# One of two raw quads through an accumulating DMA, with pairwise minima in SBUF, in an attention and gated FFN kernel on one Trainium2 core

## The chip, the cores and the metric

The kernel runs on one core of one Trainium2 chip. The metric is the device time of one execution in microseconds (us). The core's engines are named as in the profile: PE is TensorE (PEld its weight loads), DVE is VectorE, ACT is ScalarE, POOL is GpSimd, and SP issues most DMAs.

## What is computed

`x` has 2048 rows of 448 columns. Two blocks read the same `x` and are mixed by a gate of one number per row (float32 throughout):

```python
g = sigmoid((x * gate_w).sum(-1, keepdims=True))
q, k, v = split(x @ wqkv)              # 16 heads of 28
p = softmax(q @ k.T * 28 ** -0.5)      # per head, 2048 x 2048
a = (p @ v) @ wo
gate, up = x @ W_gate, x @ W_up        # 448 -> 1792
b = (relu(gate) * up) @ W_down
out = g * a + (1 - g) * b
```

## The kernel before

**Precision.** A float32 operand of the projections is split into a high part (a copy rounded to the fast matmul type, `act_high`, L102) and a low part (the rest, a subtraction: `low` on VectorE, L108, or `pool_low` on GpSimd, L111). Eleven matmuls per projection tile multiply the parts. Q and K are kept as high and low rows of one 128-row tile, together with two rows that carry a subtracted maximum.

**Stages.** A prologue computes Q, K and V (Q and K go through DRAM, `qk_d`). Then come 32 *visits* v, two per head h = v // 2, each for half of the 16 key chunks of 128 and all four query blocks of 512. Beside the attention of a visit runs a part of the FFN's gate and up projections. After the visits the rest of the FFN, the output projection and the down projection follow.

**Two ways of taking the softmax maximum.** Scores are computed transposed, keys on the partitions. For query blocks 0 to 2 the row maximum of the scores is found beforehand: `smax` (L161) computes a score tile with queries on the partitions into a PSUM pair of 128x1024 (L169), and VectorE reduces it (L171). `smax_end` (L178) transposes a head's maxima and writes them into two rows of its Q tile, so that later scores come out of TensorE with the maximum already subtracted; ScalarE evicts them by an exponential (L260). Heads are 1.5 ahead: the first m of an odd visit 2h+1 is the first that reads Q and K of head h+2. Query block 3 has no maximum beforehand. Its scores are *raw*: in each visit the first four score pairs (two *quads* of 128x2048 in SBUF) are copied raw by ScalarE (L262). `block_max` (L211) takes their elementwise maximum on VectorE, reading the PSUM pair itself, in 512-column operations (L228) into a tile `RM`. `all_max` (L232) reduces `RM` over the partitions on GpSimd (L234), `take_max` (L237) subtracts it from one quad on VectorE (L239), and `take_exp` (L242) takes the quad's exponential on ScalarE (L246). For an odd visit `RM` starts from the even visit's, and `rescale` (L574) corrects the head's even half.

**The order within a visit** is written out by hand as a string, one letter a step, and every engine executes its instructions in this order:

- s: one score pair, two matmuls (L256) and its eviction; m: one `smax` step, two matmuls and a reduction; x: one gate or up matmul (L547), 11 of them to a unit, with `relu` (L557), the product (L560) and a spill at a unit's end, and `load_f` (L536) for split weights after every second unit
- A: `all_max`; d: `take_max`; e: `take_exp`; c, f: the two parts of `rescale`; n: `smax_end` in odd visits
- w: the split of raw FFN weights that the next visits need (`split_f`, L519; 14 blocks in two parts each, so only in the early visits), with the low parts on GpSimd; u, l: special steps of the first visit
- P, Q: the two halves of the product with V (`pv`, L593), 32 matmuls each (L601), called the po block here

FIRST is the string of visit 0 (2 units), LONG of most (3 units, 33 x), WIDE has 4 units (44 x), LATE is that of the last three visits, with 4 units and no m. The scores run three pairs ahead of the visit (AHEAD), so the fourth raw pair of a visit is scored behind the po block of the visit before. Eight early scores lie in the prologue; their maxima are taken in one loop after it (L660). PSUM has three pairs for s and m together, and two single banks.

**Other queues.** `small_things` (L638) is called at a visit's start and at its eighth s. At the start of even visits it loads K and Q of head h+2 (`load_k` L146, `load_q` L151, four DMAs of 224 KB each, over SP); at the eighth s of even visits it inverts the row sums of the head before (`row_sums` L613, through `l_d` in DRAM) and spreads them back over partitions (`spread` L619, `rb`); at the start of odd visits it normalises (`normalise` L625). SP's queue is in program order: a DMA that waits holds back those behind it.

Of the kernel before, what the change touches and what calls it, by code (L numbers as in the profile page):

```python
# [37 lines left out]

EARLY = (5, 4, 4, 3, 2, 2, 1, 1)

AHEAD = 3

NP = 10

FIRST = "AmxmxsmxmxxlxsxumsmmmxxxsxdxxxsxssmxxmxsmmxdexxsxsewsPQ"

LONG = "ssmnAxxxxsmxsxmxsmxxxmsmxxxsmxxmxsdxsxxxsxsmxxxsmxxmexxsmxxdxxcsxsefwsPQ"

WIDE = "smnmxxxxxxxsxxmxxxxmsxmxxsmxxsAmxsxmxxsxsmxdxsxxsssxxxmxxxcsxmsxxdxxmxxxxexsxewsPfQ"

LATE = "snwsxxAxdxxxsxxsxxxsxxdsxxxxcsxxsxxxsxxxsxxxxsxsxxxxsxxxxxexxxsxxessPfQ"
# [15 lines left out]
def gated_mix_kernel(ctx, tc, x, wq, wo, wgu, wd, out):  # L67
# [8 lines left out]
    def f32(ap):  # L76
        return ap.bitcast(F32)
# [21 lines left out]
    def ps_x(name):  # L99
        return psum.tile([P, TB], F32, tag="x", bufs=2, name=name)  # L100
# [105 lines left out]

    stream = [p for v in range(2 * H) for p in visit(v)]
    todo_max, todo_sub, todo_exp, todo_all = [], [], [], []
    RM = {}

    def block_max(v, j, k, p, q):  # L211

        n = TQ[v // 2]
        b = j - NB + n
        if (v, b) not in RM:
            if b == 0:
                rm = att.tile([P, max(TQ), TB], F32, name=f"rm_{v}", tag=f"rm{v % 2}", bufs=1)
                for c in range(n):
                    RM[v, c] = rm[:, c]
        r = RM[v, b]  # L220
        if k % (NK // 2):
            parts = [(p[:, c], r) for c in range(2)]
        elif v % 2:
            parts = [(p[:, 0], RM[v - 1, b]), (p[:, 1], r)]
        else:
            parts = [(p[:, 0], q[:, 1])]
        for x, y in parts:
            nc.vector.tensor_tensor(r, x, y, op=OP.max)  # L228
        if k % (NK // 2) == NK // 2 - 2:
            todo_all.append((v, b, [(v, j, i) for i in (k // 4 - 1, k // 4)]))  # L230

    def all_max():  # L232
        v, b, quads = todo_all.pop(0)
        nc.gpsimd.partition_all_reduce(RM[v, b], RM[v, b], P, bass_isa.ReduceOp.max)  # L234
        todo_sub.extend((v, b, q) for q in quads)

    def take_max():  # L237
        v, b, q = todo_sub.pop(0)
        nc.vector.tensor_tensor(QUAD[q], QUAD[q], RM[v, b].unsqueeze(1).to_broadcast([P, 4, TB]), op=OP.subtract)  # L239
# [8 lines left out]
    def score(late=True):  # L248

        v, done, q, half, chunks = stream.pop(0)  # L250
        h = v // 2
        if q not in QUAD:
            QUAD[q] = p_slot(next(slots) % NP, f"P_{v}_{q[1]}_{q[2]}")
        ps = ps_w(f"s_{v}_{chunks[0][0]}_{chunks[0][1]}")
        for c, (k, j) in enumerate(chunks):
            nc.tensor.matmul(ps[:, c], K[h % 3][:, k * P:(k + 1) * P], Q[h][:, j * TB:(j + 1) * TB], start=True, stop=True)  # L256
            AT[v, k, j] = QUAD[q][:, 2 * half + c]
        dst = QUAD[q][:, 2 * half:2 * half + 2]
        if done:
            nc.scalar.activation(dst, ps, AF.Exp, scale=SCALE)  # L260
        else:
            nc.scalar.activation(dst, ps, AF.Copy)  # L262
# [25 lines left out]
    with tc.tile_pool(name="qkv", bufs=1) as pa:  # L288
# [132 lines left out]

        warm = pa.tile([P, TB], BF16, name="warm")
        nc.vector.memset(warm, 0.0)
        ps = ps_x("warm_ps")
# [51 lines left out]
        for n, (f, *a) in enumerate(mixed):  # L476
            if n == 0:
                split_w(*w5)
            if n == 6:
                load_k(1)  # L480
                load_q(1)
            if n == 8:
                split_w(*w3)
            if n == 13:

                nc.gpsimd.memset(f32(K[2])[96:128], -1.0)
            if n == len(mixed) - 6:
# [8 lines left out]
            news = [(score, False) for back in EARLY if back == len(mixed) - n]  # L496
# [161 lines left out]
    split_f(0, act_high, pool_low, (0,))  # L658
    fetch_f(1)
    while todo_max:  # L660
        block_max(*todo_max.pop(0))
    for v, (order, nu) in enumerate(ROUNDS):
        todo = list(range(nxt, nxt + nu))
        nxt += nu
        small_things(2 * v)
        passes = [(*divmod(k, 2), n) for k in todo for n in range(NT)]
        units = []
        ns = 0
        for o in order:
            if o == "x" and not passes:  # L670
                continue
            if o == "s":
                ns += 1
                if ns == 8:
                    small_things(2 * v + 1)
                if stream:
                    score()
            elif o == "m":
                if m < len(maxima):
                    smax(m)  # L680
                    m += 1
            elif o == "x":
                i, half, n = passes.pop(0)
                if n == 0:
                    units.append((i, half, ps_x(f"gu_{i}_{half}")))
                gu_mm(units[-1][2], i, half, n)
                if n == NT - 1:
                    i, half, ps = units.pop()
                    spill_h(i, ps) if half else relu(i, ps)
                    if half:  # L690
                        load_f(i + 2)
            elif o == "n":
                if v % 2 and v < 2 * H - 1:
                    smax_end(v // 2 + 1)
            elif o == "w":
                ready = nxt + (ROUNDS[v + 1][1] if v + 1 < len(ROUNDS) else 2)
                ready = min(ready + ready % 2, 2 * NF)
                while parts < ready:
                    split_f(parts // 2, act_high, pool_low, (parts % 2,))
                    parts += 1  # L700
                    if parts % 2 == 0:
                        fetch_f(parts // 2 + 1)
            elif o == "A":
                all_max()
            elif o == "d":
                take_max()
            elif o == "e":
                take_exp()
            elif o in "cf":
                rescale(v, "cf".index(o))  # L710
            elif o == "l":
                sends.pop()()
            elif o == "u":
                split_f(0, act_high, pool_low, (1,))
# [8 lines left out]
        left = [k for k in todo_exp + todo_sub + todo_all if k[0] == v]  # L723
        assert not passes and not left and v not in PO or len(stream) == max(0, 16 * (2 * H - 1 - v) - AHEAD), (v, passes, left, len(stream) + 16 * (v + 1))
    assert not stream and m == len(maxima), (len(stream), m)
    stk.close()

# [181 lines left out]
```

## Time and profile before

| | us |
|---|---|
| median of 3 runs | 1289.12 (1284.76 to 1290.27) |
| the profiled execution | 1281.88 |
| its span, first to last instruction | 1280.1 |
| prologue, up to the first steps of FIRST | 0 to about 120 |
| end of the prologue, FIRST up to its po block | 120 to 170 |
| from the first po block to the last | 170.3 to 1065.8 |
| rest of the FFN, output and down projection | from 1074 |

Durations below come from the profiled execution. A row of the grouped view reads: line, engine, operation, output<-input, shape, xcount | busy us, mean ns of one | idle time of the engine before them and what ended it. The chain is the work that ended last, followed back from the end: a start, a length and an instruction in each row. A row of the stretch view reads: stretch, length, busy us of PE, PEld, DVE, ACT, POOL with instruction counts, granted TensorE clock, DMA share, GB/s. "issue" is time in which an engine waited for nothing that the profile shows.

### The profile page before, as it was taken

To read this page: it belongs to the slowest core of one execution; us is meant where nothing else is said; L and a number is where in the kernel's file an instruction comes from. 1 tells how busy PE (TensorE), PEld (TensorE's weight loads), DVE (VectorE), ACT (ScalarE), POOL (GpSimd) and SP (SyncE) were. 2 spreads that over 40 slices of the span, in tenths; PEclk is the share of its full clock that TensorE was granted. 3 is DMA by queue.
4 is the path that set the end of the run, shared out by engine and by line. 5 is a ranking of instruction groups with operands and counts; after the bars stand their busy time and mean duration, and the time that the engine had idled before them with its cause. 6 is when DMAs were issued, how large, how long until landed. Compare 5 with 4: busy or idle time off the path is not lost.

```text
span 1280.1 us, 16867 instructions
## 1 busy us (share of the span) xinstructions
PE 1241.6 (97%) x6431; PEld 872.5 (68%) x6431; DVE 962.1 (75%) x1022; ACT 776.1 (61%) x894; POOL 191.2 (15%) x188
## 2 busy tenths in 40 slices
PE   9999699999999999999999999999999999999998
PEld 6888466665656666666666566666666566799998
DVE  6466679898988989998988889898989543563342
ACT  5223377777877677777777677767777784122121
POOL 4222221221221000000000001000000010551020
PEclk9999899999999999999999999999999999999999
DMA  9845275352626543342536243342442325745432
GB/s 323 289 189 222 84 209 117 127 163 72 169 76 201 169 121 84 103 133 64 163 104 186 81 113 103 84 130 93 132 128 76 119 90 195 228 147 159 132 115 80
DMA packets 64269, 178.37 MB, mean 139 GB/s; under 512 B 13730, under 2 KB 20578, under 8 KB 59554
## 3 DMA queue, kind: packets, MB, share of 16 engines
q1 hardware_dynamic: 57452, 151.00, 39.5%
q0 software_dynamic: 6304, 25.82, 5.3%
q8 instruction: 51, 0.84, 0.3%
q10 hardware_dynamic: 432, 0.46, 0.1%
q14 instruction: 30, 0.25, 0.1%
HBM read 118.58 MB, written 58.87 MB: 139 GB/s over the span
## 4 chain that ended last, share of the span: by engine, by line
PE 89%; DVE 4%; ACT 2%; DMA 2%; issue 1%; POOL 1%; SPq 0%; POOLq 0%; ACTq 0%
PE gu L547 19%; PE s L256 19%; PE po L601 18%; PE sm L169 13%; PE acc L808 10%; PE qk L381 5%; DVE rm L228 3%; PE wo L767 3%; PE v L399 3%; ACT P L262 1%; DVE mx L171 1%; DMA wg<-ws_d 1%; DMA or<-o_d 0%; DMA wr<-wq 0%; ACT P L260 0%
## 5 line engine op out<-in xcount | busy, mean ns | idle before, releaser
L171 DVE TENSOR_REDUCE mx<-sm 128x1 f32<-128x1024 f32 x384 | 456.5, 1219 | 60.6 <-PE sm L169 59.5
L547 PE MATMUL gu<-X,wg 128*128 128x512 f32 x1232 | 373.9, 398 | 10.8 <-POOL wg L112 7.2
L260 ACT ACTIVATE P<-s 128x1024 f32<-128x1024 f32 x306 | 306.7, 1025 | 116.8 <-PE s L256 113.1
L256 PE MATMUL s<-Q,K 128*128 128x512 f32 x1024 | 319.5, 403 | 13.6 <-DVE rm L228 11.2
L547 PEld LDWEIGHTS gu<-X,wg 128*128 128x128 f32 x1232 | 231.6, 189 | 69.1 <-POOL wg L112 7.6
L256 PEld LDWEIGHTS s<-Q,K 128*128 128x128 f32 x1024 | 184.7, 189 | 99.3 <-DVE rm L228 10.9
L169 PE MATMUL sm<-K,Q 128*128 128x512 f32 x768 | 243.2, 398 | 7.5 <-DVE mx L171 3.6
L601 PE MATMUL po<-P,V 128*32 128x512 f32 x1640 | 227.3, 594 | 0.0
L228 DVE TENSOR_TENSOR rm<-s,rm 128x512 f32<-128x512 f32 x218 | 150.4, 690 | 74.6 <-ACT P L262 57.3
L169 PEld LDWEIGHTS sm<-K,Q 128*128 128x128 f32 x768 | 137.1, 188 | 52.6 <-ACT P L260 10.1
L234 POOL PARTITION_ALL_REDUCE rm<-rm x32 | 57.2, 1788 | 673.7 <-DVE rm L228 618.8
L601 PEld LDWEIGHTS po<-P,V 128*32 128x32 f32 x1640 | 62.6, 110 | 116.2 <-issue 111.5
L808 PE MATMUL acc<-WD,hh 128*128 128x448 f32 x672 | 138.5, 365 | 0.0
L262 ACT ACTIVATE P<-s 128x1024 f32<-128x1024 f32 x104 | 105.1, 1024 | 46.6 <-PE s L256 45.4
L808 PEld LDWEIGHTS acc<-WD,hh 128*128 128x128 f32 x672 | 126.2, 188 | 10.4
L239 DVE TENSOR_TENSOR P<-P,rm 128x2048 f32<-128x2048 f32 x52 | 117.9, 2272 | 5.8 <-POOL rm L234 5.8
L601 PE MATMUL po<-V 128*32 128x512 f32 x408 | 115.0, 594 | 0.0
L103 ACT ACTIVATE hh<-hr 128x512 fp32r<-128x512 f32 x56 | 35.2, 631 | 117.8 <-PE acc L808 113.8
L246 ACT ACTIVATE P<-P 128x2048 f32<-128x2048 f32 x52 | 99.4, 1914 | 5.3 <-DVE P L239 4.5
L260 ACT ACTIVATE V<-s 128x1024 f32<-128x1024 f32 x78 | 78.9, 1025 | 37.1 <-PE s L256 35.2
L109 DVE TENSOR_TENSOR hh<-hr,hh 128x512 fp32r<-128x512 f32 x56 | 49.4, 883 | 62.2 <-ACT hh L103 62.2
L381 PE MATMUL qk<-X,W 128*128 128x512 f32 x308 | 77.4, 398 | 0.3 <-DVE X L109 0.2
(79 smaller groups left out, 772.4 us busy)
## 6 DMA issues: line engine op xcount, KB each, us to landing
wg<-ws_d SPq DMA_DIRECT2D x42, 896.0 KB
K<-qk_d SPq DMA_DIRECT2D x64, 224.0 KB
Q<-qk_d SPq DMA_DIRECT2D x64, 224.0 KB
h_d<-h SPq DMA_DIRECT2D x56, 256.0 KB
hr<-h_d SPq DMA_DIRECT2D x56, 256.0 KB
ws_d<-wg SPq DMA_DIRECT2D x14, 896.0 KB
qk_d<-st POOLq DMA_DIRECT2D x21, 512.0 KB, 3.2
wgr<-wgu SPq DMA_DIRECT2D x13, 512.0 KB
```

Of the source, the lines that this page charges most:

```text
L169: nc.tensor.matmul(ps[:, c, :], Q[h][:, u * P:(u + 1) * P], K[h % 3][:, k0:k0 + TB], start=True, stop=True)
L171: nc.vector.tensor_reduce(MX[h][:, 2 * u + half:2 * u + half + 1], ps, axis=AX.XY, op=OP.max)
L228: nc.vector.tensor_tensor(r, x, y, op=OP.max)
L239: nc.vector.tensor_tensor(QUAD[q], QUAD[q], RM[v, b].unsqueeze(1).to_broadcast([P, 4, TB]), op=OP.subtract)
L246: nc.scalar.activation(q, q, AF.Exp, scale=SCALE)
L256: nc.tensor.matmul(ps[:, c], K[h % 3][:, k * P:(k + 1) * P], Q[h][:, j * TB:(j + 1) * TB], start=True, stop=True)
L260: nc.scalar.activation(dst, ps, AF.Exp, scale=SCALE)
L262: nc.scalar.activation(dst, ps, AF.Copy)
L381: nc.tensor.matmul(ps, W[:, a, c * P:(c + 1) * P], xf(tb, b), start=(n == 0), stop=(n == NT - 1))
L547: nc.tensor.matmul(ps, WS[i][:, s, a], xf(i // NF, b), start=(n == 0), stop=(n == NT - 1))
L601: nc.tensor.matmul(po[32 * j:32 * j + 32], V[:, h // 4 % 2, k, h % 4], AT.pop((v, k, j)), start=(k == k0), stop=(k == k0 + NK // 2 - 1))
L808: nc.tensor.matmul(ACC[i // NF][t][:, :D], HH[i][:, a, t * P:(t + 1) * P], WD[:, f, b], start=(f == 0 and n == 0), stop=(f == NF - 1 and n ...
```

## The change

Seven things change, in one diff.

1. The raw copies are negated (scale -1), and the exponential's scale is negated. The maximum becomes a minimum of negated scores, taken by a new step b (`block_min`): three operations over 1024 SBUF columns per visit (the first of two raw pairs, two that add one pair each), one over the halves, and then a negation (even visits) or a negation and maximum with the even visit's `RM` (odd visits). It no longer reads PSUM. The loop that takes the early pairs' maxima is gone; b steps in FIRST take them.
2. `take_max` has two ways: g, on VectorE as before (an addition now), and d, an accumulating DMA from GpSimd's queue that adds `RM`, read four times over, to the quad in SBUF. FIRST has two g; the other strings have one g and one d.
3. AHEAD is 4: all four raw pairs of a visit are scored before the po block of the visit before.
4. The low parts of the FFN weights are taken on VectorE in the visits.
5. A partition all-reduce of a small tile is issued on GpSimd in the prologue.
6. K and Q of head h+2 are loaded in the middle of an even visit, behind `row_sums` and `spread`; the middle is the tenth s.
7. The zero rows of the third Q tile come by two DMAs from zero rows of another Q tile; the order strings are new, and WIDE is used for visits 3, 8, 11 and 20 (before: 3, 10, 17 and 24).

```diff
-AHEAD = 3
+AHEAD = 4
-LONG = "ssmnAxxxxsmxsxmxsmxxxsmsxxxsmxxmxsdxsxxxsxsmxxxsmxxmexxsmxxdxxcsxsefwsPQ"
+LONG = "smnsxxmxxsmxxmxAsxmxxxsmxsxxsxxgsxxxsmsxxdmxsxxsmscxxxsmxmxxxexssebxmbmbwfPQ"
...
-ROUNDS = [(FIRST, 2)] + [(WIDE, 4) if k % 7 == 2 else (LONG, 3) for k in range(2 * H - 4)] + [(LATE, 4)] * 3
+ROUNDS = [(FIRST, 2)] + [(WIDE, 4) if k in (2, 7, 10, 19) else (LONG, 3) for k in range(2 * H - 4)] + [(LATE, 4)] * 3
...
+    def block_min():
+
+        if not todo_max:
+            return
+        v, j, p = todo_max[0]
+        b = j - NB + TQ[v // 2]
+        if (v, b) not in R2:
+            R2[v, b] = att.tile([P, 2, TB], F32, name=f"r2_{v}_{b}", tag="r2", bufs=1)
+            left[v, b] = NK // 4 - 2
+            nc.vector.tensor_tensor(R2[v, b], todo_max.pop(0)[2], todo_max.pop(0)[2], op=OP.min)
+            return
+        nc.vector.tensor_tensor(R2[v, b], R2[v, b], todo_max.pop(0)[2], op=OP.min)
+        left[v, b] -= 1
+        if left[v, b]:
+            return
+        r, r2 = att.tile([P, TB], F32, name=f"rm_{v}_{b}", tag=f"rm{v % 2}{b}", bufs=1), R2[v, b]
+        RM[v, b] = r
+        nc.vector.tensor_tensor(r, r2[:, 0], r2[:, 1], op=OP.min)
+        if v % 2:
+            nc.vector.scalar_tensor_tensor(r, r, -1.0, RM[v - 1, b], op0=OP.mult, op1=OP.max)
         else:
+            nc.vector.tensor_scalar(r, r, -1.0, None, op0=OP.mult)
...
-    def take_max():
+    def take_max(way):
         v, b, q = todo_sub.pop(0)
-        nc.vector.tensor_tensor(QUAD[q], QUAD[q], RM[v, b].unsqueeze(1).to_broadcast([P, 4, TB]), op=OP.subtract)
+        m = RM[v, b].unsqueeze(1).to_broadcast([P, 4, TB])
+        if way == "d":
+            nc.gpsimd.dma_start(QUAD[q], m, accum_op=OP.add)
+        else:
+            nc.vector.tensor_tensor(QUAD[q], QUAD[q], m, op=OP.add)
         todo_exp.append(q)
...
-        nc.scalar.activation(q, q, AF.Exp, scale=SCALE)
+        nc.scalar.activation(q, q, AF.Exp, scale=-SCALE)
...
-            nc.scalar.activation(dst, ps, AF.Copy)
-            job = (v, chunks[0][1], chunks[0][0], ps if late else dst, dst)
-            if late:
-                block_max(*job)
-            else:
-                todo_max.append(job)
+            nc.scalar.activation(dst, ps, AF.Copy, scale=-1.0)
+            todo_max.append((v, chunks[0][1], dst))
...
+        nc.gpsimd.partition_all_reduce(warm_r, warm_r, P, bass_isa.ReduceOp.max)
...
-        if q == 0 and h and h + 2 < H:
-            load_k(h + 2)
-            load_q(h + 2)
...
             spread(h - 1)
+            if h + 2 < H:
+                load_k(h + 2)
+                load_q(h + 2)
...
-                if ns == 8:
+                if ns == 10:
                     small_things(2 * v + 1)
...
-                    split_f(parts // 2, act_high, pool_low, (parts % 2,))
+                    split_f(parts // 2, act_high, low, (parts % 2,))
...
-                nc.gpsimd.memset(f32(QS[2])[96:128], 0.0)
+                for a, b in ((GD, 12), (GD + 12, 4)):
+                    nc.sync.dma_start(f32(QS[2])[a:a + b].rearrange("p j t -> p (j t)"), Q[1][GD + 2:GD + 2 + b].bitcast(F32))
```

The other strings after the change:

```python
FIRST = "lsbssxmmmxxsbsmmxumxsbssxmxsAxmxxgxxxxsxmxxxmmxgbmxsexxbwesPbQ"
WIDE = "nsssAxxxcxxxxsmxsxxmxsmxfxsxmxsxmxxsdsgxxxsxxxxsmxxsmxxmxxsmbxxxsxmxembxxxxxxxmesxPwbQ"
LATE = "nsssxAxxxxsgxxxcxsxxxxsxsxxxsxxwxsxxxsxxxsxssxxxxxdxxexsxxxxsexxsbxxxbPbfQ"
```

More of the change, by code (lines that the diff above doesn't have):

```diff
@@ L39 @@
 EARLY = (5, 4, 4, 3, 2, 2, 1, 1)
-AHEAD = 3
+AHEAD = 4
 NP = 10
[L45 to L51, printed above, removed]
-ROUNDS = [(FIRST, 2)] + [(WIDE, 4) if k % 7 == 2 else (LONG, 3) for k in range(2 * H - 4)] + [(LATE, 4)] * 3
+FIRST = "lsbssxmmmxxsbsmmxumxsbssxmxsAxmxxgxxxxsxmxxxmmxgbmxsexxbwesPbQ"
+LONG = "smnsxxmxxsmxxmxAsxmxxxsmxsxxsxxgsxxxsmsxxdmxsxxsmscxxxsmxmxxxexssebxbmbwfPQ"
+WIDE = "nsssAxxxcxxxxsmxsxxmxsmxfxsxmxsxmxxsdsgxxxsxxxxsmxxsmxxmxxsmbxxxsxmxembxxxxxxxmesxPwbQ"
+LATE = "nsssxAxxxxsgxxxcxsxxxxsxsxxxsxxwxsxxxsxxxsxssxxxxxdxxexsxxxxsexxsbxxxbPbfQ"
+ROUNDS = [(FIRST, 2)] + [(WIDE, 4) if k in (2, 7, 10, 19) else (LONG, 3) for k in range(2 * H - 4)] + [(LATE, 4)] * 3
 TERMS = [(0, 0), (3, 0), (1, 1), (4, 1), (2, 2), (5, 2), (6, 3), (0, 4), (1, 5), (2, 6), (6, 7)]
@@ L208, in gated_mix_kernel @@
     todo_max, todo_sub, todo_exp, todo_all = [], [], [], []
[L209 to L224, printed above, removed]
-        else:
[L226 to L230, printed above, removed]
+    RM, R2, left = {}, {}, {}
+    def block_min():
[17 more added lines that the diff above has]
+            nc.vector.scalar_tensor_tensor(r, r, -1.0, RM[v - 1, b], op0=OP.mult, op1=OP.max)
+        else:
+            nc.vector.tensor_scalar(r, r, -1.0, None, op0=OP.mult)
+        q = NK // 8 * (v % 2)
+        todo_all.append((v, b, [(v, j, q), (v, j, q + 1)]))
     def all_max():
@@ L245, in take_exp, with score @@
         q = QUAD[q].rearrange("p c t -> p (c t)")
-        nc.scalar.activation(q, q, AF.Exp, scale=SCALE)
-    def score(late=True):
+        nc.scalar.activation(q, q, AF.Exp, scale=-SCALE)
+    def score():
         v, done, q, half, chunks = stream.pop(0)
@@ L423, in gated_mix_kernel @@
         nc.vector.memset(warm, 0.0)
+        warm_r = pa.tile([P, 16], F32, name="warm_r")
+        nc.vector.memset(warm_r, 0.0)
         ps = ps_x("warm_ps")
@@ L495, in gated_mix_kernel @@
                 m += 1
-            news = [(score, False) for back in EARLY if back == len(mixed) - n]
+            news = [(score,) for back in EARLY if back == len(mixed) - n]
             for k, c in enumerate(news):
@@ L654, in small_things @@
             spread(h - 1)
+            if h + 2 < H:
+                load_k(h + 2)
+                load_q(h + 2)
         if h and q == 2:
             normalise(h - 1)
-    split_f(0, act_high, pool_low, (0,))
+    split_f(0, act_high, low, (0,))
     fetch_f(1)
-    while todo_max:
-        block_max(*todo_max.pop(0))
     for v, (order, nu) in enumerate(ROUNDS):
@@ L722, in gated_mix_kernel @@
                 pv(v, "PQ".index(o))
-        left = [k for k in todo_exp + todo_sub + todo_all if k[0] == v]
-        assert not passes and not left and v not in PO or len(stream) == max(0, 16 * (2 * H - 1 - v) - AHEAD), (v, passes, left, len(stream) + 16 * (v + 1))
+        rest = [k for k in todo_exp + todo_sub + todo_all if k[0] == v]
+        assert not passes and not rest and v not in PO or len(stream) == max(0, 16 * (2 * H - 1 - v) - AHEAD), (v, passes, rest, len(stream) + 16 * (v + 1))
     assert not stream and m == len(maxima), (len(stream), m)
```

8 lines of the change are left out of this document (5 added, 3 removed).

## The prediction

> **What bounds the kernel now.** I read the page first: busy time, then the chain that ended last.
>
> ```profile
> span 1280.1 us, 16867 instructions
> PE 1241.6 (97%) x6431; PEld 872.5 (68%) x6431; DVE 962.1 (75%) x1022; ACT 776.1 (61%) x894; POOL 191.2 (15%) x188
> PE 89%; DVE 4%; ACT 2%; DMA 2%; issue 1%; POOL 1%; SPq 0%; POOLq 0%; ACTq 0%
> ```
>
> TensorE is busy for 97% but holds 89% of the chain: its ends are modelled, and some of its busy time is waiting. The chain gives DVE 4% and ACT 2%, about 77 us, and that is what a change on VectorE can reach. Where do they lie? The chain in order of time, over the whole span:
>
> ```profile
> 170.32 7.24 PE po L601 x64
> ...
> 1038.50 1.87 PE gu L547 x8
> ...
> 1065.84 7.87 PE po L601 x64
> ```
>
> Each visit ends in one po block of 64 matmuls, 7.0 us. A 512-column matmul takes 1.87/8 = 0.234 us. LONG holds 16 s and 12 m of two matmuls each and 33 x: 89 x 0.234 + 7.00 = 27.8. WIDE (100 matmuls) needs 30.4, LATE (76) 24.8. From the first po block to the last are 31 visits, 24 LONG, 4 WIDE and 3 LATE: 863 us of work in 1065.84 - 170.32 = 895.5. So 32 us are lost, 1.0 a visit, and a LONG visit takes about 28.9. The chain of one visit shows the place:
>
> ```profile
> 325.99 1.04 ACT P L262
> 327.03 0.03 issue
> 327.06 0.70 DVE rm L228
> 327.76 0.02 issue
> 327.78 0.70 DVE rm L228
> 328.48 0.14 issue
> 328.62 0.70 PE s L256 x2
> 329.32 0.46 PE sm L169 x2
> ```
>
> Right behind the po block the fourth raw pair is copied by ScalarE (L262), then VectorE reads the same PSUM pair twice for the maximum (L228); only then is the pair free for the next s. The s behind the pause takes 0.70 instead of 0.46: about 0.23 us of filling per visit (7 us in all) that comes with any break. 32 - 7 = 25 us hang on this.
>
> The second place is FIRST. The stretch as a whole (its last three columns: granted clock, DMA share, GB/s), TensorE's longest wait, the chain there, and GpSimd's side of the all-reduce line:
>
> ```profile
> 119.70:177.50 57.80, 45.59 (x204) 30.21 (x202) 36.17 (x40) 29.07 (x39) 12.87 (x15) 0.88 0.39 116
> ```
> ```profile
> PE gu L547 <- POOL wg L112: 7.2, 1, 7.2
> ```
> ```profile
> 135.68 0.70 DVE rm L228
> ...
> 142.61 1.07 PE sm L169 x2
> ...
> 149.45 6.58 issue
> 156.04 0.98 POOL wg L112
> ```
> ```profile
> L234 POOLq MODIFY_POOL_CONFIG  x18: 1/6/16, 138.7 to 386.7; - x18
> ```
>
> 204 matmuls, 64 of them po, are 140 x 0.234 + 7 = 40 us of work in 57.8: 18 us lost. The early raw pairs' maxima are taken in one run from 135.68, and the m behind them starts only at 142.61; then a low part on GpSimd starts only at 156.04, after 6.6 us in which the trace shows nothing that it waits for. Pool configurations are loaded 18 times, and only while low parts and all-reduces alternate, so I read that gap as such a load. After each pause two matmuls take 1.07 instead of 0.46 for a few us, and the granted clock of the stretch is 0.88: some 4 us more.
>
> **The change part by part.** Durations, by group of one shape:
>
> ```profile
> L171 DVE TENSOR_REDUCE mx<-sm 128x1 f32<-128x1024 f32 x384 | 456.5, 1219 | 60.6 <-PE sm L169 59.5
> L228 DVE TENSOR_TENSOR rm<-s,rm 128x512 f32<-128x512 f32 x218 | 150.4, 690 | 74.6 <-ACT P L262 57.3 <-ACT V L262 10.0 <-DVE rm L228 0.5
> L239 DVE TENSOR_TENSOR P<-P,rm 128x2048 f32<-128x2048 f32 x52 | 117.9, 2272 | 5.8 <-POOL rm L234 5.8
> L109 DVE TENSOR_TENSOR X<-xr,X 128x1024 fp32r<-128x1024 f32 x6 | 7.3, 1224 | 3.6 <-ACT X L103 3.5
> L627 DVE TENSOR_TENSOR os<-os,rb 128x512 f32<-128x512 f32 x16 | 11.6, 724 | 0.0
> L109 DVE TENSOR_TENSOR W<-wr,W 128x336 fp32r<-128x336 f32 x6 | 2.8, 504 | 2.0 <-ACT W L103 1.9
> L106 DVE CAST WO<-wor 128x448 fp32r<-128x448 f32 x1 | 0.4, 382 | 0.0
> ```
>
> *Maxima.* Gone: 7 or 8 operations a visit (7.5 x 0.69 = 5.2 us). New: three minima over 1024 columns of SBUF (X row, 1.22 each), one over 512 (L627 row, 0.72) and a negation or negate-and-maximum over 512. The last has no row: 0.38 (the cast) to 0.72; I take 0.6. Sum 5.0 us, so VectorE's work stays the same and only its place moves: a PSUM pair is free after ScalarE's 1.03 us, and all four raw pairs are scored ahead of the po block. What is late next behind the block is ScalarE's and VectorE's own queue.
>
> *Subtractions.* 64 of 2.27 us become 33 (two in FIRST, one in each other visit): -70 us on VectorE. The 31 others become DMAs from GpSimd's queue; below.
>
> *Low parts.* 28 of 128x384 go to VectorE: between the W row and the X row, 0.55 each, and 14 smaller ones at about 0.42: +21 us, all in FIRST and the first eight or nine visits, 2.3 us a visit there. So VectorE gains nothing in these visits (2.27 given, 2.3 taken) and 2.3 us in the later ones. GpSimd loses them, and they bounded nothing there but the single 7.2 us wait; it has no more alternation, so no pool loads between its all-reduces. The warming all-reduce pays one such load while GpSimd's first stores, not TensorE, wait behind it: nothing, or the 6.6 us if a store held back qk's staging tiles; three of these are free at that time, so I take nothing.
>
> *The accumulating DMAs.* No accumulate is in this trace. GpSimd issues it right behind its all-reduce; behind it are queued only a small memset and the next visit's all-reduce, so its wait holds up nothing near. The third minimum ends about when the po block does, so the issue falls 2 to 3 us into the visit. The exponential that needs it stands 20 us in (LONG) and its po half 24 us in: 17 to 21 us of cover. Its price, 1 MB each:
>
> ```profile
> x_d<-X POOLq DMA_DIRECT2D x6, 1024.0 KB, 5.1
> ```
> ```profile
> 853.71 1.76 SPq L148 DMA_DIRECT2D K<-qk_d  x4
> ...
> 867.00 0.34 SPq L539 DMA_DIRECT2D wg<-ws_d  x1
> 867.44 0.38 SPq L617 DMA_DIRECT2D l_d<-rq  x1
> 871.97 1.72 SPq L623 DMA_DIRECT2D rb<-l_d  x4
> ```
> ```profile
> 853.70:864.40 10.70, 10.61 (x45) 7.72 (x44) 9.59 (x10) 5.70 (x7) 1.83 (x2) 1.00 0.80 172
> 864.40:867.00 2.60, 2.60 (x13) 2.08 (x12) 2.48 (x4) 2.00 (x3) 0.00 (x0) 1.00 0.04 13
> ```
>
> Lower end: a plain 1 MB store from the same queue, 5.1 us. Upper end: the loads of K and Q (eight of 224 KB, 1.8 MB, issued from 853.71, the queues idle again from 864.4: 10.7 us, 6 us a MB) three times over, for two reads and a write: 18 us. I take 10, twice the nearest row, wholly hidden; uncovered from about 20, and then every visit pays.
>
> *K and Q loads.* They leave the start of even visits and queue on SP behind the row sums: In the rows above l_d is issued 13.7 us behind the first K load, about 15 us into the visit, and rb 4.5 us later, since l_d stood behind wg in its queue. In the new order the wg load of such a visit mostly comes after: TensorE reaches the tenth s at 11.9, a reduction and the reciprocal follow, l_d at 13.5, rb at 15 to 18, K at 17 to 20, all landed 10.7 us later, at 27.6 to 30.5. The first m that reads them is the second step of the next visit, at 28.5, and TensorE takes its steps in order. The reason that I lean to the early end: the DMA queues are idle then (share 0.04 between the loads above), and l_d should land in about 1.5 us. I charge 0.5 us in each of the 11 odd LONG visits concerned: 5 us.
>
> *The rest.* The negating copies are the same ScalarE instructions with another scale, and the exponential takes the sign back: nothing. The zero rows of the third Q tile come by two small DMAs on SP ahead of head 2's loads instead of a memset: SP was idle there for 20 us, nothing; if those loads came 2 us late, head 2's first m would wait, after the po block of FIRST. Four raw pairs ahead instead of three fill the two free quads of ten: no extra wait, since their slots are those of the visit before last. WIDE visits move to 3, 8, 11 and 20, four as before: nothing by themselves, but two of them are the long even ones, two the odd ones whose first m stands 4 us later, so 9 to 11 pairs remain for the K and Q charge.
>
> **A page against it.** The Trainium skill, "DMA: Bandwidth & Descriptors", section "Issuing engines are not separate DMA queues", says that transfers from all queues share the same 16 engines and interleave; by it an accumulate still in flight at 17 us would stretch the K and Q loads. The 0.80 share for 10.7 us agrees that these loads leave little room. This is the first rival's other way in, and it moves its chance, not the sum.
>
> **Sum.** Of the 25 us at the visits' starts, eight visits keep about 0.9 (VectorE no freer there, and its low parts fall into the po block): 18 left. Queue jitter behind the block, 0.1 a visit: 15. K and Q: -5, so 10. FIRST becomes bound by VectorE: 12 reductions (14.6), five minima and the closing pair (7.4), two subtractions (4.5), one low part: 27.5 us of work from 135.7, of which the last 2 can lie beside the po block, so po starts near 161 instead of 170.3: 9 us, between 0 (VectorE's queue jams the m) and 15 (all but the clock). The rest, the later stage with DMA waits from 1074 us, is left alone. Together -19, and with the ends 0 and -40. In its own time the profiled execution takes 1281.9 (span 1280.1 plus 1.8); 1263. The runs' median, 1289.1, lies 7.2 above it: **1270 us**.
>
> **The rivals.**
> 1. *K and Q late* (no gain). If l_d again takes 4.5 us, or an accumulate shares the engines, the loads land 2 to 3 us after the m needs them, in 11 visits: +22 to +33. 1270 - 5 + 28 = 1293 at 2.5 us. For it: a margin of 0.9 us at best; the first nine visits also move the FFN weights, raw and split. Against: it starts only behind 28.5. Chance 0.2.
> 2. *The accumulate outlasts its cover* (slower). The place is ScalarE's second exponential of a visit; behind it on ScalarE wait the copies that free PSUM, and behind these TensorE. It decides at about 20 us; at 22 each of 31 visits pays 2: 1270 + 62 = 1332. For it: no row shows an accumulate, and the upper end is 18. Against: 10 is twice the nearest row. Chance 0.18.
> 3. *The wait only changes its name.* The pair is free after ScalarE, but the m behind it wait for VectorE's reductions, 12 x 1.22 of 28 us; the visits stay at 28.9 and FIRST alone gives 9: 1280. Chance 0.1.
> 4. *More than forecast*: visits at 28.0 and FIRST at its 15: 1250. Chance 0.12.
>
> **How the numbers follow.** Forecast 1255 to 1282: chance 0.4. Faster by over 0.5% (under 1282.7; 0.5% is about what can be told from no change here): forecast, rival 4 and most of rival 3: 0.6. Within: the rest of 3 and half of 1: 0.17. Slower: rival 2 and the upper tail of 1: 0.23. The range 1246 to 1310 leaves out the best of rival 4 and rival 2 from 21.3 us on.
>
> **What would show it.** Right: no VectorE maximum of raw pairs in the chain behind the po blocks; LONG starts 28.1 to 28.4 apart after the ninth visit; 33 subtractions; the accumulates land in 7 to 14 us and no exponential waits for them; no gap before low parts in FIRST, with the first po near 161. Wrong: ScalarE idle for a DMA into P, or TensorE's weight loads for m waiting on K or Q at the start of odd visits.

## The result and the profile after

The changed kernel takes 1272.83 us (median of 4 runs, 1271.43 to 1278.62) against 1287.33 of the kernel before (4 runs beside it): a ratio of 0.9895, 95% interval 0.9854 to 0.9936. The forecast was 1270. The profiled execution takes 1271.51 us, 10.4 less than the one of before; the median fell by 14.5, because before's profiled execution was 5.4 under this median of four runs (7.2 under the median of three that the forecast started from) and the new one is 1.3 under its own. What follows explains the 10.4; the forecast had 19.

The page of the kernel after: span, busy time, shares of the chain, and the new DMA (count, KB, median us from issue to landing).

```profile
span 1269.6 us, 16730 instructions
PE 1238.6 (98%) x6431; PEld 876.4 (69%) x6431; DVE 913.8 (72%) x954; ACT 771.8 (61%) x894; POOL 201.8 (16%) x177
PE 79%; DMA 10%; DVE 5%; ACT 2%; SPq 2%; issue 1%; POOL 1%; ACTq 0%; DVEq 0%; POOLq 0%
P<-rm POOLq DMA_DIRECT2D x27, 1024.0 KB, 9.1
```

VectorE lost 48 us, near the 49 of the forecast (70 given to DMAs, 21 taken by low parts). The share to look at is DMA, up from 2% to 10% of the chain. That share isn't a loss: a transfer on the chain counts with its whole length, and TensorE works through most of it. Between the first po block and the last, TensorE's own idle time is about 17 us before and after. What changed is what it waits for: VectorE and ScalarE before, mostly transfers after. One LONG visit (visit 10) in the chain, from po block to po block:

```profile
434.61 7.00 PE po L608 x64
441.62 0.65 PE s L264 x2
...
462.51 3.55 PE po L608 x29
```

No VectorE or ScalarE piece stands behind this block any more; only the 0.65 of the first s is left of the break. The visit lasts 462.51 - 434.61 = 27.9 us, where 27.8 is its matmuls' own time. Reading all 32 po blocks this way gives, for each kind of visit, a length that most visits share (the *floor*) and what single visits take above it:

| us | before | after |
|---|---|---|
| first po block starts | 170.3 | 161.3 |
| floor of LONG, of WIDE | 28.9, 31.0 | 27.9, 30.5 |
| 31 visits at their floors (24 LONG, 4 WIDE, 3 LATE) | 891.3 | 864.5 |
| above the floor, in single visits | 4.2 | 28.3 |
| first po block to last | 895.5 | 892.8 |
| last po block to the end | 214.3 | 215.5 |

So the visits' floor gave 26.8 us, more than forecast, and single visits took 24.1 back. Those with most above the floor are visit 1 (31.4), 3 (36.3, WIDE), 6 (30.0), 8 (34.3, WIDE), and the odd ones 13, 17, 19, 23 and 25 (28.9, 32.0, 29.0, 29.7, 29.9).

**An odd visit: K and Q.** SP's queue in visit 16, which begins at 613.3; then the chain (visit 17 begins inside it), and TensorE's timeline with the idle time in brackets:

```profile
626.82 0.32 SPq L624 DMA_DIRECT2D l_d<-rq  x1
629.78 1.71 SPq L630 DMA_DIRECT2D rb<-l_d  x4
631.54 1.68 SPq L148 DMA_DIRECT2D K<-qk_d  x4
633.97 1.74 SPq L155 DMA_DIRECT2D Q<-qk_d  x4
```
```profile
634.90 7.52 DMA Q<-qk_d
642.41 1.68 issue
644.09 0.99 PE sm L169 x2
...
645.30 0.85 PE s L264 x2
...
647.86 0.46 PE gu L554 x2
```
```profile
644.09 0.99 PE L169 MATMUL sm<-K,Q 128*128 128x512 f32 x2 [2.23 <-issue]
```

The last load on the chain lands 29.1 us behind the visit's start; the s ahead of the m that needs the loads ends at 28.6. TensorE idles 2.23 us. Of these, 1.68 lie behind that landing and are "issue", so what they wait for isn't shown. Its pairs of matmuls then take 0.99 once and 0.85 three times, instead of 0.46, until 647.9: another 1.7, at a granted clock of 0.57 (third column from the end). So this lateness is paid almost twice. Visit 17 is the exception, though: in visits 13, 19, 23 and 25 TensorE pauses for 0.7 to 1.75 us and then takes 0.70 once, which is the filling, and 0.46 from there on. The stretch behind the pause of visit 17, and the longest of the other four pauses:

```profile
644.00:648.00 4.00, 3.91 (x11) 2.91 (x12) 1.51 (x3) 1.60 (x3) 0.00 (x0) 0.57 1.05 298
```
```profile
876.46 0.70 PE L169 MATMUL sm<-K,Q 128*128 128x512 f32 x2 [1.75 <-DMA Q<-qk_d]
```

**Early visits: bursts on SP.** In visit 3 the chain waits for the Q rows with the maxima (L188, two of 8 KB); in visit 8 for the row sums, 8 KB, which SP issues behind two stores of split weights (L539):

```profile
236.74 8.96 DMA Q<-mh
...
245.84 1.19 PE s L264 x2
247.03 0.85 PE sm L169 x2
```
```profile
383.22 10.22 DMA ls<-os
...
393.47 0.07 DVE rq L623
```
```profile
380.19 1.83 SPq L539 DMA_DIRECT2D ws_d<-wg  x2
383.22 0.64 SPq L618 DMA_DIRECT2D ls<-os  x1
```

These small transfers take 9 and 10 us. In visit 8 it is VectorE, which works in order, that stands at the reciprocal (L623) with the m reductions behind it.

**FIRST.** Its stretch, to be read beside the 57.8 us of before, and the chain at its po block:

```profile
119.70:172.00 52.30, 45.58 (x207) 28.25 (x206) 40.78 (x47) 30.28 (x41) 5.10 (x7) 0.97 0.51 148
```
```profile
155.59 9.40 DMA wgr<-wgu
...
166.40 1.81 ACT P L254
...
168.25 3.62 PE po L608 x26
```

The block starts 8.9 us earlier, at a clock of 0.97 instead of 0.88, but in its middle TensorE waits for an exponential that stands behind a weight split on ScalarE, which waits for raw weights. The block lasts 10.6 instead of 7.2: the 3.5 us of visit 1 are these.

### The profile page after: what moved, and what is told of

The parts are those of the page before. It is cut to its first block, busy times and chain, and to the rows that moved or that the text cites. A ratio compares the mean times of both kernels' runs of the same rounds, so it can differ in the third digit from the quotient of the medians.

```text
span 1269.6 us, 16730 instructions
## 1 busy us (share of the span) xinstructions
PE 1238.6 (98%) x6431; PEld 876.4 (69%) x6431; DVE 913.8 (72%) x954; ACT 771.8 (61%) x894; POOL 201.8 (16%) x177
## 4 chain that ended last, share of the span: by engine, by line
PE 79%; DMA 10%; DVE 5%; ACT 2%; SPq 2%; issue 1%; POOL 1%; ACTq 0%; DVEq 0%; POOLq 0%
PE gu L554 19%; PE s L264 16%; PE sm L169 12%; PE po L608 11%; PE acc L816 10%; PE qk L385 5%; PE wo L775 3%; PE v L403 3%; DMA h_d<-h 2%; DMA K<-qk_d 2%; DVE mx L171 1%; DMA Q<-qk_d 1%; DMA wg<-ws_d 1%; ACT P L254 1%; DVE wg L109 1%
## 5 line engine op out<-in xcount | busy, mean ns | idle before, releaser
L171 DVE TENSOR_REDUCE mx<-sm 128x1 f32<-128x1024 f32 x384 | 462.3, 1221 | 135.4 <-PE sm L169 132.8
L554 PE MATMUL gu<-X,wg 128*128 128x512 f32 x1232 | 378.2, 399 | 3.4 <-DMA wg<-ws_d 3.4
L268 ACT ACTIVATE P<-s 128x1024 f32<-128x1024 f32 x306 | 303.5, 1025 | 114.9 <-PE s L264 107.0
L554 PEld LDWEIGHTS gu<-X,wg 128*128 128x128 f32 x1232 | 234.3, 190 | 60.3 <-DMA wg<-ws_d 3.7
L238 POOL PARTITION_ALL_REDUCE rm<-rm x32 | 67.6, 2113 | 780.6 <-DVE rm L230 390.3
L816 PEld LDWEIGHTS acc<-WD,hh 128*128 128x128 f32 x672 | 126.2, 188 | 10.4
L270 ACT ACTIVATE P<-s 128x1024 f32<-128x1024 f32 x104 | 104.1, 1023 | 29.1 <-PE s L264 26.3
L268 ACT ACTIVATE V<-s 128x1024 f32<-128x1024 f32 x78 | 78.6, 1024 | 29.1 <-PE s L264 27.5
L567 DVE TENSOR_TENSOR h<-gu,rl 128x512 f32<-128x512 f32 x56 | 38.2, 683 | 46.8 <-ACT rl L564 18.9
L385 PEld LDWEIGHTS qk<-X,W 128*128 128x128 f32 x308 | 57.9, 189 | 15.4 <-DVE X L109 1.2
```

The lines of the kernel that those rows point to most:

```text
L171: nc.vector.tensor_reduce(MX[h][:, 2 * u + half:2 * u + half + 1], ps, axis=AX.XY, op=OP.max)
L270: nc.scalar.activation(dst, ps, AF.Copy, scale=-1.0)
L385: nc.tensor.matmul(ps, W[:, a, c * P:(c + 1) * P], xf(tb, b), start=(n == 0), stop=(n == NT - 1))
L554: nc.tensor.matmul(ps, WS[i][:, s, a], xf(i // NF, b), start=(n == 0), stop=(n == NT - 1))
L816: nc.tensor.matmul(ACC[i // NF][t][:, :D], HH[i][:, a, t * P:(t + 1) * P], WD[:, f, b], start=(f == 0 and n == 0), stop=(f == NF - 1 and n ...
```

## The experiments

Labels that begin with b are edits of the kernel before, those with a of the kernel after; each ratio is to the kernel before, run on the same chip.

**Is it the held PSUM pair?** b_sbuf takes the late maxima from the SBUF copy, and so frees the pair after ScalarE:

```diff
-            job = (v, chunks[0][1], chunks[0][0], ps if late else dst, dst)
+            job = (v, chunks[0][1], chunks[0][0], dst, dst)
```

> The kernel before with one edit: VectorE takes the maxima of the raw pairs from ScalarE's copy in SBUF, as many operations of as many columns, so that a PSUM pair is free after the copy. Theory A (the held pair costs the 1.0 us a visit): the pause behind the po blocks shrinks from about 2.6 us to about 1.0, LONG visits go from 28.9 to 28.2 to 28.5, and the whole is 12 to 20 us faster than before. Theory B (VectorE's load holds the visits, the wait only changes its name): LONG visits stay within 0.2 us of 28.9, the whole within 6 us of before.

1291.88 us, ratio 1.0056 (1.0035 to 1.0077). Most LONG visits stay at 28.8 to 28.9; visits 1, 3, 4, 6 and 8 are 0.8 to 3.3 us longer than before. TensorE's longest wait from 430 to 1060 us (who for whom: us in total, times, longest), in the kernel before and in b_sbuf:

```profile
PE s L256 <- DVE rm L228: 8.1, 11, 0.8
```
```profile
PE s L256 <- DVE mx L171: 7.6, 12, 0.7
```

The chain behind a po block of b_sbuf, and VectorE's timeline there:

```profile
484.02 0.46 PE sm L169 x2
...
485.53 0.47 PE s L256 x2
486.00 1.21 DVE mx L171
...
487.25 0.73 PE s L256 x2
```
```profile
484.64 1.42 DVE L228 TENSOR_TENSOR rm<-P,rm 128x512 f32<-128x512 f32 x2 [2.59 <-ACT P L262]
485.98 1.22 DVE L171 TENSOR_REDUCE mx<-sm 128x1 f32<-128x1024 f32 x1
```

The two maxima no longer hold a PSUM pair, but VectorE still executes them right there, ahead of the reduction of the first m. That m's matmuls end at 484.48 and its reduction starts only at 485.98, and an s waits for it. In a few visits a ScalarE eviction ends last instead. The wait changed its name, as the prediction's rival 3 has it, and kept its length.

**Is it VectorE's load?** b_skip leaves out the second quad's subtraction in visits 1 to 31 (nothing takes its place); b_skip_sbuf does that and b_sbuf's edit.

```diff
-        nc.vector.tensor_tensor(QUAD[q], QUAD[q], RM[v, b].unsqueeze(1).to_broadcast([P, 4, TB]), op=OP.subtract)
+        if v == 0 or q[2] % 2 == 0:
+            nc.vector.tensor_tensor(QUAD[q], QUAD[q], RM[v, b].unsqueeze(1).to_broadcast([P, 4, TB]), op=OP.subtract)
```

> The kernel before with the subtraction of the second raw quad left out in visits 1 to 31 (that quad's exponential is taken of unsubtracted scores), so that VectorE has 2.27 us less to do in a visit and nothing else changes. Theory B (VectorE's load is what holds the visits): LONG visits go from 28.9 to 27.9 to 28.3, the whole 15 to 28 us faster than before. Theory A, in what is left of it (the held pair is a wait of its own): LONG visits stay at 28.6 or more, since the pair is still held behind the po block.

> The same with the maxima taken from ScalarE's copy in SBUF as well (the subtraction of the second quad is left out as before). If VectorE's load alone holds the visits: as with the subtraction left out alone, within 0.2 us a visit. If the freed pair pays once VectorE has room: LONG visits 0.3 to 0.8 us shorter than with the subtraction left out alone, 27.9 to 28.1.

b_skip: 1285.72 us, ratio 1.0005 (0.9988 to 1.0022), LONG visits mostly at 28.9. b_skip_sbuf: 1288.84, ratio 1.0024 (1.0012 to 1.0036), most of them at 28.7 to 28.9. From 430 to 1060 us TensorE's longest wait in b_skip is that of the kernel before, and in b_skip_sbuf that of b_sbuf, each to a tenth of a us:

```profile
PE s L257 <- DVE rm L228: 8.1, 11, 0.8
```
```profile
PE s L257 <- DVE mx L171: 7.6, 12, 0.7
```

Freeing the pair, relieving VectorE, and both together: none gives anything in the old order, which keeps two maxima right behind the block.

**Then is it the new order alone?** a_all_g keeps everything of the change but the accumulates: all quads go through VectorE (d becomes g in LONG, WIDE and LATE).

```diff
-LONG = "smnsxxmxxsmxxmxAsxmxxxsmxsxxsxxgsxxxsmsxxdmxsxxsmscxxxsmxmxxxexssebxmbmbwfPQ"
+LONG = "smnsxxmxxsmxxmxAsxmxxxsmxsxxsxxgsxxxsmsxxgmxsxxsmscxxxsmxmxxxexssebxmbmbwfPQ"
...
```

> The changed kernel with every subtraction on VectorE, no accumulating DMA: 31 operations of 2.27 us more on VectorE. Theory A (the freed pair is the gain, VectorE's relief is not needed in most visits): even LONG visits stay at 27.9 to 28.4, the pauses of odd visits stay or shrink since the DMA engines are freer, the whole 1262 to 1282. Theory B (VectorE's relief is the gain): LONG visits go back to 28.7 or more, the whole 1285 to 1300.

1296.41 us, ratio 1.0087 (1.0069 to 1.0104): 24 us above the changed kernel and slower than before. LONG visits mostly take 29.3 to 30.4, and the break stands behind the second subtraction, where the reductions on VectorE come late. The chain there shows ScalarE's evictions; over 430 to 1060 us TensorE waits longest for the reductions:

```profile
521.96 1.96 ACT P L268 x2
...
523.96 0.72 PE sm L169 x2
```
```profile
PE sm L169 <- DVE mx L171: 12.6, 9, 1.7
```

So the 26.8 us of the floor need both: the new order, and the accumulating DMA that takes 2.3 us a visit off VectorE. What in the new order does it wasn't tried apart: the four pairs ahead, the strings and the minima from SBUF came together. And a_all_g keeps strings that were laid out for one subtraction on VectorE, so an order that carries two of them isn't ruled out.

**What does the accumulate cost?** a_skip_d leaves the accumulates out (their quads keep unsubtracted scores):

```diff
-            nc.gpsimd.dma_start(QUAD[q], m, accum_op=OP.add)
+            pass
```

> The changed kernel with the accumulating DMAs left out (the second quad's exponential, in WIDE the first's, is taken of unsubtracted scores), so that the order and VectorE's relief stay and the traffic of 31 MB goes. Theory: the visits' floor is 27.9 as with the DMAs, so the accumulates cost nothing at their own place; odd visits keep a pause of 0 to 2 us since K and Q come as late; visits 3 and 8 shrink by 1 to 3 us: the whole 4 to 15 us faster than the changed kernel. Rival (the accumulates are what makes the loads late): odd visits at 27.9 to 28.1, the whole 15 us or more faster.

1260.75 us, ratio 0.9819 (0.9789 to 0.9849). The floor is the same 27.9, so at their own place the accumulates cost nothing, and it is VectorE's relief that counts, not the DMA that brings it. What goes is mostly in three visits: 3 (36.3 to 30.6), 8 (34.3 to 30.5), 17 (32.0 to 28.8), 12.7 us in all. The other odd visits stay as they were (28.9, 29.4, 29.2, 29.4 in visits 13, 19, 23, 25). The section "Issuing engines are not separate DMA queues" of the Trainium skill's "DMA: Bandwidth & Descriptors", by which transfers from all queues run on the same 16 engines and interleave, agrees with the three visits that fell; in the other odd visits the accumulates make no difference that could be seen.

**K and Q: when should they be loaded?** a_kq_start moves the loads back to the start of even visits; a_kq5 to the fifth s.

```diff
+        if q == 0 and h and h + 2 < H:
+            load_k(h + 2)
+            load_q(h + 2)
...
-            if h + 2 < H:
-                load_k(h + 2)
-                load_q(h + 2)
```

> The changed kernel with K and Q of head h+2 loaded at the start of an even visit again. Theory A (the visits gave 12 us back because these loads land behind the m that read them): odd LONG visits come down to 27.9 to 28.2 and the whole is 6 to 14 us faster than the changed kernel, 1259 to 1267; the accumulates of even visits land in 12 to 18 us instead of 9, still before their exponential. Rival (the accumulate then outlasts its cover): ScalarE waits for a DMA into P in even visits, and the whole is no faster than 1270 or up to 1300.

> The changed kernel with K and Q of head h+2 loaded at the fifth s of an even visit, ahead of the row sums. Theory (late loads): odd LONG visits at 27.9 to 28.1 as with the loads at the visit's start, but the accumulates are past most of their way: 9 to 12 us to landing in the median, not 13.7; the whole 1258 to 1268. Rival: the accumulates are held up as much and visits of even number grow, 1268 or more.

a_kq_start: 1268.22 us, ratio 0.9873 (0.9835 to 0.9910). a_kq5: 1275.87, ratio 0.9926 (0.9909 to 0.9944). Both miss the range of their theory, and both ratios lie within the interval of the changed kernel. Yet in both the odd visits 5, 7, 13, 17, 19, 23 and 25 fall to 27.9 to 28.0: the position of the loads was the cause of their pauses. But visit 9 rises to 37.1 and 37.9, from 28.0. a_kq_start's chain and SP queue in visit 9:

```profile
416.89 11.86 DMA X<-x_d
```
```profile
398.53 0.34 SPq L624 DMA_DIRECT2D l_d<-rq  x1
408.38 1.71 SPq L630 DMA_DIRECT2D rb<-l_d  x4
```

rb, which reads l_d back, is issued almost 10 us behind it, and the reload of x (L558), queued on SP behind rb, comes too late. The pause has moved, not gone. (Visit 27 of a_kq5 takes 33.4, but it isn't shown that the loads are the reason: a_no_warm, below, which differs from the changed kernel by one instruction of the prologue, has 32.9 there, and 30.1 and 29.9 in visits 9 and 15 against 28.0 and 28.5. So up to about 4 us in one visit of one execution can come without an edit near it.) The accumulates too are stretched: from issue to landing in a_kq_start, then in the changed kernel,

```profile
DMA to landing us min/median/max: 7.7/12.4/21.8
```
```profile
DMA to landing us min/median/max: 7.7/9.1/15.8
```

**Is it SP's order in the early visits?** a_ws_pool issues the stores of split weights from GpSimd's queue.

```diff
-            nc.sync.dma_start(ws_d[i], f32(w))
+            nc.gpsimd.dma_start(ws_d[i], f32(w))
```

> The changed kernel with the stores of the split FFN weights (0.9 MB each, visits 0 to 8) issued from GpSimd's queue instead of SP's. Theory (small DMAs wait in SP's order behind these stores: the rows of maxima in visit 3, the row sums in visit 8): visits 3 and 8 shrink from 36.3 and 34.3 by 2 to 4 us each, the whole 4 to 10 us faster than the changed kernel. Rival (all share the same DMA engines, the queue doesn't matter): visits 3 and 8 within 1 us of these.

1276.21 us, ratio 0.9925 (0.9907 to 0.9942). Visits 3 and 8 fall to 31.2 and 30.4, about as they did without the accumulates. So each pause goes when either goes, the stores ahead in SP's queue or the accumulates: it takes both to make it. (The edit moves the accumulates too: they come behind the stores in GpSimd's queue.) But visit 1 takes 37.2 (FIRST's po block 16.4, where TensorE waits for raw weights) and visit 9 35.4, and the whole isn't faster than the changed kernel, against the theory's 4 to 10 us.

**The low parts, and the warming all-reduce.** b_low takes the low parts on VectorE in the kernel before (`pool_low` becomes `low` in the three `split_f` calls of the visits); a_pool_low puts them back on GpSimd in the kernel after; a_no_warm removes the all-reduce in the prologue.

> The kernel before with one edit: the low parts of the FFN weights in the visits on VectorE instead of GpSimd. Theory A: GpSimd no longer alternates, the 6.6 us gap in FIRST goes and the first po block starts 5 to 8 us earlier; visits 1 to 8 get 2.3 us more of VectorE and lengthen by 0.5 to 1.5 us each, so that the whole is between 8 us faster and 4 us slower. Rival (the gap is something else than a pool load): the first po block starts within 2 us of 170.3, the whole 4 to 12 us slower.

> The changed kernel with the low parts in the visits on GpSimd again. Theory: GpSimd alternates between low parts and all-reduces again, so the accumulates of visits 1 to 8 are issued 6 to 15 us later; the first po block starts 0 to 7 us later than 161.3; visits 1 to 8 have 2.3 us less on VectorE but wait for late accumulates or late weights: the whole between 3 us faster and 15 us slower than the changed kernel, visits from 9 on unchanged.

> The changed kernel without the all-reduce in the prologue. Theory: with the low parts on VectorE GpSimd has nothing to alternate with and is idle for over 10 us ahead of its first all-reduce, so the pool load is hidden: first po block at 161 to 162, the whole within 4 us. Rival (the warming pays): the first all-reduce comes about 6 us later and the first po block at 165 to 168.

b_low: 1284.06 us, ratio 0.9988 (0.9977 to 0.9998). The first po block comes 5.6 us earlier (164.6); visits 6, 8 and 9 give it back (30.2, 30.1, 33.4, against 28.9, 28.9 and 29.3; what holds visit 9 wasn't followed, and b_skip has 31.5 there). a_pool_low: 1293.44, ratio 1.0053 (1.0033 to 1.0074), 20 us above the changed kernel and so more than any expectation. Visits 3, 5, 7 and 9 take 41.2, 33.6, 33.4 and 36.3; from visit 10 on none is more than 0.4 us longer. GpSimd's timeline, idle time in brackets, and the chain a little later:

```profile
165.07 7.94 POOL L112 TENSOR_TENSOR wg<-wgr,wg 128x384 fp32r<-128x384 f32 x6 [9.46 <-ACT wg L103]
178.96 1.80 POOL L238 PARTITION_ALL_REDUCE rm<-rm  x1 [5.94 <-ACT P L268]
...
205.95 1.80 POOL L238 PARTITION_ALL_REDUCE rm<-rm  x1 [5.73 <-DVE mx L171]
```
```profile
271.41 6.24 issue
277.65 1.81 POOL rm L238
279.49 2.29 DVE P L247
```

Each all-reduce behind low parts starts about 6 us late, and VectorE stands at the g step for it. The Trainium skill's "GPSIMD Engine Reference", section "Instruction dispatch", tells of some 6 us at the first call of a freshly loaded kernel, with no instruction to be seen; the 5.7 to 6.8 us ahead of the all-reduces here agree, and come at every alternation. a_no_warm: 1270.17, ratio 0.988 (0.9859 to 0.9901), first po block at 161.6: with the low parts away, the warming gains nothing that can be measured.

**A version from these.** a_best2 loads K and Q at the fifth s in visits 4, 12, 16, 18, 22 and 24 alone, where x reloads do not suffer, and behind the row sums elsewhere; FIRST's last e stands ahead of its w.

```diff
-            if h + 2 < H:
+            if h + 2 < H and u // 2 not in FIFTH:
...
+                if ns == 5 and v in FIFTH:
+                    load_k(v // 2 + 2)
+                    load_q(v // 2 + 2)
```

> The changed kernel with K and Q at the fifth s in the even LONG visits 4, 12, 16, 18, 22 and 24 only (not where the load of the next x block or of V stands behind them), and in FIRST the second exponential ahead of the split that waits for raw weights. Theory (late loads): visits 5, 13, 17, 19, 23 and 25 at 27.9 to 28.1, the po block of FIRST at 7.1 instead of 10.6, no other visit over 1 us longer than in the changed kernel: the whole 10 to 15 us faster than the changed kernel, 1258 to 1263. Rival (the pauses only move on, as with all loads at the fifth s): 1268 or more.

1261.06 us (1260.25 to 1268.19), ratio 0.9826 (0.9799 to 0.9853), the fastest complete version; its interval ends just below that of the changed kernel. The profiled execution took 1267.14, so the visits are those of a slower one of its runs. Visits 13, 19, 23 and 25 take 28.0, 28.0, 28.5 and 27.9, and visit 9 stays at 28.0. Visit 17 takes 29.3, not the 27.9 to 28.1 expected, and visit 27, 29.7 (28.5 in the changed kernel). Visits 3 and 8 keep their 36.6 and 34.3. The edit of FIRST gained nothing: its block is 8.9 long but starts at 163.8, and ends at 172.7 instead of 171.9.

## Why the prediction came out as it did

The direction was right, and so was much of the mechanism, but that the median came within 3 us of 1270 is partly luck: large errors of the sum cancel, and of the rest most is hidden by how far the old profiled execution lay under its median.

- **The visits' starts, forecast -15 (25 less 7 for early visits and 3 of jitter).** Measured -26.8 at the floor: nearly the whole loss, with most of the filling and with the WIDE and early visits. The two raw maxima did leave the chain. But the step "a PSUM pair is free after ScalarE's 1.03 us" was not the cause by itself. Freed alone (b_sbuf) or with VectorE relieved (b_skip_sbuf), the visits stay at 28.8; the new order with all subtractions on VectorE (a_all_g) takes them to 29.3 and more. The chain named the wait that came last; behind it stood another of the same length, the m's reduction that VectorE starts only behind the same two maxima (7.6 us over 12 pauses in b_sbuf, where the held pair made 8.1 over 11). Rival 3, given 0.1, is what the old order does.
- **"So VectorE gains nothing in these visits", 0.9 kept in eight early visits.** Wrong: visits 2, 4 and 5 take 28.3, 27.9 and 28.2. Where early visits lose much, in 3 and 8, they lose it to DMAs.
- **K and Q, forecast +5.** Measured 12.7 above the floor in odd visits 5 to 27, 11.3 of it in the seven that an earlier load brings to the floor (a_kq_start). The sign that the prediction named for being wrong, an m that waits for K or Q, was seen. The times up to the issue were right: l_d at 13.5 us in most even visits, rb 1.4 to 1.5 behind it in eleven of thirteen, K at 16.7, the early end. Too small was the 10.7 for the loads themselves, taken at a visit's start in the old kernel: the m of visits 13, 17, 19, 23 and 25 start 12.2 to 13.6 us behind the first issue of K. In a_skip_d it is 12.2 to 13.1 in the same visits, so the accumulates aren't the main reason; what lengthens the loads wasn't isolated. Visit 17, with 4.1 us, has more: rb came 3.0 behind l_d, and the rate was halved behind the pause. The accumulates, rival 1's second way in, made up to 3.2 of these 4.1 (a_skip_d).
- **Early visits, no term.** 15.7 us in visits 1, 2, 3, 6 and 8 were not in the sum. In visits 3 and 8 the runs show SP's order and the accumulates together; visit 1 is FIRST's block, and visits 2 and 6 were not told apart. The rule of the Trainium skill that the prediction cites was weighed for the K and Q loads alone, and not for the small transfers that queue behind stores.
- **FIRST, forecast -9 with po "near 161".** Measured -8.9, at 161.3. The load of pool configurations was read rightly (b_low alone gives 5.6). What is late next, ScalarE's exponential in the po block, was not followed. And the prediction reads the rows of FIRST loosely: the pair takes 1.07 once, filling included, and 0.85 behind it, and this follows the two long pauses there, not each.
- **The accumulates, forecast 10 us and hidden.** Measured 9.1 (7.7 to 15.8) under a cover of 17 to 21. This group shows ScalarE's idle time ahead of the exponentials in its last column:

```profile
L254 ACT ACTIVATE P<-P 128x2048 f32<-128x2048 f32 x52 | 99.2, 1913 | 0.3
```

- **VectorE's counts.** Per visit three minima of 1.22, one of 0.69, and a negation or negate-and-maximum: 4.9 us against the 5.0 forecast. The low parts are dearer than the 0.55 worked out (25 us in all instead of 21), which VectorE's groups show beside the maxima:

```profile
L222 DVE TENSOR_TENSOR r<-r,P 128x1024 f32<-128x1024 f32 x52 | 63.3, 1218 | 2.5 <-ACT P L270 1.3
L228 DVE TENSOR_TENSOR rm<-r 128x512 f32<-128x512 f32 x32 | 22.1, 692 | 1.1
L109 DVE TENSOR_TENSOR wg<-wgr,wg 128x384 fp32r<-128x384 f32 x26 | 18.3, 747 | 0.2
L232 DVE TENSOR_SCALAR rm<-rm 128x512 f32<-128x512 f32 x16 | 6.8, 427 | 0.5
```

- **The 7.2 between profile and median** did not carry over (1.3 after). These 5.9 us hide most of the 8.5 by which the profiled time missed 1263, and that is luck.

## What to carry to other kernels

A wait that the chain shows is only the last of several: before it is priced, ask what stands behind it, and if two waits have one length, removing one gives nothing. When a change moves work to DMAs, follow every small transfer of the early, busy part of the kernel through its queue; a few KB behind a 0.9 MB store, with another large transfer in flight, can stop an engine that works in order. And charge a pause of TensorE by more than its length where the rate falls behind it, which here began at pauses of about 2 us.

## What the runs showed of the hardware

- A 1 MB accumulate from SBUF to SBUF lands in 9.1 us, where the plain 1 MB store from the same queue took 5.1; issuing it holds GpSimd for 1.3 us.
- Behind a pause of 2.23 us TensorE ran two matmuls in 0.85 us instead of 0.46 for some 4 us. The Trainium skill's "TensorE: Matmul & The Clock Gate", Part 1, gives an idle window of about 3.4 us for this; the shorter pause was enough here. In the changed kernel the pauses of 2.07 and 2.81 did the same and none up to 1.75 did; in a_kq_start a pause of 2.75 in visit 8 did not.
- A transfer of 8 KB took 10.2 us behind two stores of 0.9 MB in its queue, with an accumulate in flight. That fits the section "Queues, rings and completion order" of the Trainium skill's "DMA: Bandwidth & Descriptors", by which an engine takes the descriptors of one ring in order; but without the accumulates (a_skip_d) VectorE did not wait for this transfer.
- The all-reduce takes 2.15 us in the changed kernel's median where it took 1.78 before; without the accumulates it still takes 2.08 (a_skip_d, a_all_g), so most of the rest has another reason, which was not isolated.
